# One down-projection over all sixteen token tiles, with seven of its eight tile pairs by Strassen's algorithm

## The chip, the cores and the metric

The kernel runs on one core of a Trainium2 chip. The core has five instruction streams: PE (TensorE, matrix products into the 8 banks of PSUM), DVE (VectorE), ACT (ScalarE), POOL (GpSimd) and SP (SyncE, which issues every DMA here). Work that depends on another stream waits on a semaphore. The metric is the time of one execution on the device in microseconds (us); lower is better. A time is the median of several runs. The profiler records one further execution, and its own time stands beside its span in the table below.

## The reference

The program is one transformer block over 2048 tokens of width 1024: layer norm, a segmented attention with a compressive memory (32 heads, 4 segments of 512 tokens), an output projection, a second layer norm and a gated feed-forward part with 3584 hidden columns.

```python
x = A_x                                        # [1, 2048, 1024]
h = x + _A_ref(_layernorm(x), A_wq, A_wk, A_wv, A_wo, A_beta)
h2 = h + _B_ref(_layernorm(h), B_w1, B_w3, B_w2)

def _B_ref(x, w1, w3, w2):                     # w1, w3: [1024, 3584]; w2: [3584, 1024]
    gate = jnp.einsum('bsd,df->bsf', x, w1)
    up = jnp.einsum('bsd,df->bsf', x, w3)
    h = _silu(gate) * up
    out = jnp.einsum('bsf,fd->bsd', h, w2)
    return out
```

In `_A_ref`, each segment does causal softmax attention within itself, adds what it retrieves from the memory of the earlier segments, and the result goes through `wo`. Inputs and output are bf16.

## The kernel before

The tokens form 16 tiles of 128, and two blocks of 1024 (tiles 0 to 7 and 8 to 15). The 3584 hidden columns form 14 chunks of 256 (`ch`), or 28 groups of 128 (`fc`, or `n` in the second block). `hnT[s]` holds the layer-normed rows of segment s, transposed; `h_scr` in DRAM holds the residual rows `h`, of which a tile is later read back into a buffer `hr`.

Every operation is first noted as an `Op` with its engine, its dependences and a cost; then `schedule` fixes the order on each engine and `emit` writes it out. For the first part of the program the order is a table of numbers (`ORDER`), so written out by hand. `BEHIND` inserts operations behind a numbered one. Operations created while `G.clock` is set are *planned*: they are sorted on their engine by that clock. `LATER` gives such a clock to some operations of the table. A wait is always for what the order and the dependences ask; a stream runs strictly in order.

The stages, with names that come back below:

- **Attention with the first up-projection.** Segments 0 to 3 of the attention are interleaved on TensorE with the up-projection of block 0 (`ffn_up`): per chunk the weights `w1b` and `w3b` are loaded (two buffers of each, used in turn), and four *units* follow, each 16 matmuls of 128x128x512 into two banks. ScalarE takes the gate (`sg`, line 1448), VectorE makes the product in two instructions and writes it to a hidden tile `hm[fc]`, [128, 1024] bf16. The 28 hidden tiles lie in SBUF as `hmA` (25) and `hmB` (3). In between `wo_stage(s)` projects a segment's attention output, adds the residual, does the layer norm and transposes by DMA; `wo_stage(3)` does it for the last segment.
- **First down-projection**, `ffn_down(0, ...)`: 8 token tiles x 2 halves x 28 matmuls = 448, with `w2` resident as `w2a`. Each tile adds `hr` and stores half rows through `ob`.
- **Weight scales**, `weight_scale`, beside it: the second up-projection works with f16 sums of the weights, so it scales w1 and w3 (one number for each) and w2 (one number) by powers of two. For that the squares of all weights are summed: ScalarE squares a piece with `accum_out` into a column of `sq` (`squares`, line 1421), for chunks 8 to 13 from the buffers of the first block, for chunks 0 to 7 from a second load into the `wide` buffers. A matmul with `ones` adds the partitions up, GpSimd takes the power -1/2 (line 1560), and VectorE keeps the exponent and makes the reciprocal (lines 1564 to 1566).
- **Second up-projection**, `products7`, block 1: Strassen's algorithm over 2x2 blocks, so seven products of four matmuls in place of eight, for each of the 28 groups (784 matmuls). `token_sums` makes the sums of the tokens (`S`) once; VectorE makes the sums of the weights (`T`, line 1609) for each group after ScalarE has scaled the chunk (line 1600); GpSimd multiplies w2 by its scale in the meantime (line 1639).
- **Second down-projection**, `down7`: the first pair of token tiles (8 and 9) as in block 0 by 112 matmuls, during which VectorE makes the sums of w2 (`Td`); then three pairs by Strassen's algorithm, 7 x 14 = 98 matmuls each. For each pair VectorE makes four sums of the hidden tiles (`pair_sums`, into `Sd`) and the combinations in `uu`, `ww` and `qq`; `ha` and `hb` are the pair's two residual tiles in `hr`.

The matmul helper `mms` is line 776 and the dense DMA helper line 407 in every view; the layer norm (`ln`) has the square of a whole row block at line 889.

Of the kernel before, what the change touches and what calls it, by code (L numbers as in the profile page):

```python
# [7 lines left out]
AF = mybir.ActivationFunctionType  # L8
# [178 lines left out]
    "6576575675675675675677565107316576556756756756756401646765645112176123477516566067147512"  # L187
    "624046476574174210464562016467")
# [10 lines left out]
    1704: 6.0, 1865: 5.1, 1866: 5.11, 1867: 5.12, 1868: 5.13, 1869: 7.2, 1870: 7.9, 1871: 8.6,  # L199
    1879: 10.5, 1880: 10.51, 1883: 12.6, 1884: 13.3, 1885: 14.0,  # L200
# [4 lines left out]
BEHIND = {8: (1733, 1733), 9: (1749, 1726), 10: (1779, 1756), 11: (1793, 1809), 12: (1832, 1832),  # L205
          13: (1876, 1853)}
# [63 lines left out]
class Graph:  # L270
# [7 lines left out]
    DMA_FIX = 1900.0  # L278

# [143 lines left out]
    def schedule(self):  # L423
# [4 lines left out]
        order = {}  # L428
        for e in ENGINES:
# [12 lines left out]
            order[e] += sorted((o for o in ops if e in o.engs and o.plan is not None),  # L442
                               key=lambda o: (o.plan, o.seq))
# [28 lines left out]
        for _ in self.ops:  # L472
            best = None
            for e in ENGINES:
                if heads[e] == len(order[e]):
                    continue
                o = order[e][heads[e]]
                if any(d not in done for d in o.deps):
                    continue
                t = max([free[e]] + [d.end if d.eng == e == "pe" else done[d] for d in o.deps])  # L480
# [16 lines left out]


# [97 lines left out]
class Kernel:  # L596
# [13 lines left out]
    def plan(self):  # L610
# [80 lines left out]
        for i, off in enumerate((r2, r2 + 8192)):  # L691
# [36 lines left out]
        assert ring >= wo + 6144 + 4096
        self.T = [buf(f"T{i}", [128, 16, 128], F16, ring + 4096 * i) for i in range(2)]
        self.S = [buf(f"S{i}", [128, 4, 512], F16, base[self.hnT[0].name][1] + 4096 * i)  # L730
                  for i in range(4)]
        hn0 = base[self.hnT[0].name][1]
        t1, t2, t4 = (buf(f"Td{i}", [128, 14, 512], F16, hn0 + 14336 * i)[:, :, :]
# [6 lines left out]
                   for i in range(3)]  # L740
        self.hd = g.dram("h_scr", [2048, 1024], BF16)
# [675 lines left out]
    def squares(self, src, n, early=0):  # L1417

        out, to = self.sq[:, n:n + 1], self.junk2[early]
        src, to = (t.rearrange("p c n -> p (c n)") for t in (src, to))  # L1420
        return self.g.op("act", act_ns(2048) + 190, lambda e, gr: [e.activation(
            to, src, AF.Square, accum_out=out)], reads=[src], writes=[to, out])

    def ffn_up(self, blk, ch):
# [468 lines left out]
```

## Time and profile before

| what | value |
|---|---|
| median of 3 runs | 850.92 us (850.85 to 851.23) |
| profiled execution, its own time | 851.94 us |
| its span, first to last instruction | 850.2 us |
| matmuls | 5645 |
| granted TensorE clock | 1.000 |
| bytes moved by DMA | 111.01 MB |
| second up-projection | 590.7 to 759.9 us |
| second down-projection | 759.9 to 847.6 us |

A page of the profile lists the busy time of each engine, the span in slices, the DMA queues, the chain of work that ended last and the costliest groups of instructions. A row of the timeline or of a group reads: start and length in us, engine, line, operation, output<-inputs with their shapes (partitions x elements); where the engine was idle before, the idle time stands in brackets with the instruction that ended it. "PEld" is TensorE's weight load, which runs beside the matmuls. A share of busy time is a mean over stages with different limits; which engine limits a stage is read from that stage. The profiled execution took 1.0 us longer than the median of the runs.

### The profile page before, as it was taken

To read this page: it belongs to the slowest core of one execution; us is meant where nothing else is said; L and a number is where in the kernel's file an instruction comes from. 1 tells how busy PE (TensorE), PEld (TensorE's weight loads), DVE (VectorE), ACT (ScalarE), POOL (GpSimd) and SP (SyncE) were. 2 spreads that over 40 slices of the span, in tenths; PEclk is the share of its full clock that TensorE was granted. 3 is DMA by queue.
4 is the path that set the end of the run, shared out by engine and by line. 5 is a ranking of instruction groups with operands and counts; after the bars stand their busy time and mean duration, and the time that the engine had idled before them with its cause. 6 is when DMAs were issued, how large, how long until landed. Compare 5 with 4: busy or idle time off the path is not lost.

```text
span 850.2 us, 13983 instructions
## 1 busy us (share of the span) xinstructions
PE 845.0 (99%) x5645; PEld 381.7 (45%) x5645; DVE 551.0 (65%) x906; ACT 483.3 (57%) x520; POOL 295.0 (35%) x288
## 2 busy tenths in 40 slices
PE   8999999999999999999999999999999999999998
PEld 5443434444444444444444444444444444444444
DVE  5777886876757677856445522312888888888443
ACT  4878677667757565532343139991777777730000
POOL 1535244425244262510200000001777777750000
DMA  7798966836893626458628279310233323201011
GB/s 235 193 213 207 236 134 182 185 90 179 210 206 91 165 61 165 112 177 217 202 74 236 59 164 304 119 33 25 59 91 99 99 66 85 75 0 51 17 49 59
DMA packets 159663, 111.01 MB, mean 131 GB/s; under 512 B 46832, under 2 KB 145392, under 8 KB 158576
## 3 DMA queue, kind: packets, MB, share of 16 engines
q1 hardware_dynamic: 159600, 110.13, 49.5%
q8 instruction: 44, 0.72, 0.4%
q14 instruction: 19, 0.16, 0.1%
HBM read 90.19 MB, written 9.44 MB: 117 GB/s over the span
## 4 chain that ended last, share of the span: by engine, by line
PE 99%; DMA 1%; SPq 0%; issue 0%; DVE 0%; DVEq 0%
PE ps L776 92%; PE ps L1148 3%; PE ps L1241 3%; DMA wp<-in_A_wk_dram 1%; PE ps L1069 0%; PE ps L1365 0%; SPq L407 0%; PE ps L1234 0%; PE ps L788 0%; DVE ob L1752 0%; DVEq L554 0%
## 5 line engine op out<-in xcount | busy, mean ns | idle before, releaser
L1162 ACT ACTIVATE et<-ps 128x2048 bf16<-128x2048 f32 x80 | 150.1, 1876 | 47.7 <-PE ps L1148 45.8
L776 PE MATMUL ps<-w2a,hmA 128*128 128x512 bf16 (+2 forms) x597 | 129.1, 371 | 0.1
L1171 POOL TENSOR_SCALAR_AFFINE_SELECT et<-et 128x512 bf16<-128x512 bf16 (+1 forms) x96 | 83.0, 876 | 112.3 <-ACT et L1162 112.3
L776 PE MATMUL ps<-hnT,w1b 128*128 128x512 bf16 x448 | 108.1, 379 | 0.0
L776 PE MATMUL ps<-hnT,w3b 128*128 128x512 bf16 x448 | 107.8, 379 | 0.0
L1448 ACT ACTIVATE sg<-ps 128x512 bf16<-128x512 f32 x56 | 33.4, 596 | 97.0 <-PE ps L776 95.7
L776 PEld LDWEIGHTS ps<-w2a,hmA 128*128 128x128 bf16 x597 | 57.5, 98 | 67.1 <-issue 0.5
L1639 POOL TENSOR_SCALAR w2a<-w2a,sc 128x1024 bf16<-128x1024 bf16 x28 | 79.7, 2848 | 7.0 <-PE ps L776 7.0
L776 PE MATMUL ps<-S,T 128*128 128x512 f16 x336 | 81.7, 379 | 0.0
L1451 DVE SCALAR_TENSOR_TENSOR t<-sg,ps 128x512 bf16<-128x512 bf16 x56 | 38.2, 684 | 63.9 <-ACT sg L1448 63.8
L776 PEld LDWEIGHTS ps<-hnT,w1b 128*128 128x128 bf16 x448 | 42.6, 98 | 52.5 <-issue 3.7
L776 PEld LDWEIGHTS ps<-hnT,w3b 128*128 128x128 bf16 x448 | 42.6, 98 | 52.4 <-issue 3.1
L1643 POOL TENSOR_TENSOR c<-uu,ww 128x512 bf16<-128x512 f32 x28 | 45.6, 1628 | 48.9 <-DVE uu L1634 48.9
L776 PE MATMUL ps<-xnT,wp 128*128 128x512 bf16 (+1 forms) x352 | 60.9, 321 | 1.3 <-DMA wp<-in_A_wk_dram 1.3
L776 PE MATMUL ps<-wo,oT 128*128 128x512 bf16 x256 | 61.1, 380 | 0.0
L776 PE MATMUL ps<-hnT,wp 128*128 128x512 bf16 x256 | 59.7, 380 | 0.0
L776 PE MATMUL ps<-hnT,wide 128*128 128x512 bf16 x224 | 57.5, 379 | 0.0
L747 ACT ACTIVATE wide<-wide,sc 128x2048 bf16<-128x2048 bf16 x28 | 55.6, 1991 | 0.0
L776 PEld LDWEIGHTS ps<-S,T 128*128 128x128 f16 x336 | 32.9, 98 | 39.6
L1456 DVE SCALAR_TENSOR_TENSOR hmA<-t,ps 128x512 bf16<-128x512 bf16 x50 | 34.0, 683 | 18.8 <-PE ps L776 18.5
L1187 DVE TENSOR_TENSOR sum<-sum,et 128x512 bf16<-128x512 bf16 (+1 forms) x64 | 40.6, 642 | 6.1 <-POOL et L1171 3.8
L1649 DVE SCALAR_TENSOR_TENSOR cc<-ps,sc,uu 128x1024 bf16<-128x1024 f32 x28 | 35.9, 1284 | 11.2 <-PE ps L776 11.2
(183 smaller groups left out, 1296.3 us busy)
## 6 DMA issues: line engine op xcount, KB each, us to landing
wide<-in_B_w_dram SPq DMA_DIRECT2D x19, 512.0 KB, 4.0
wide<-in_B_w_dram SPq DMA_DIRECT2D x38, 256.0 KB, 4.5
wp<-in_A_wv_dram SPq DMA_DIRECT2D x8, 1024.0 KB, 5.9
wp<-in_A_wq_dram SPq DMA_DIRECT2D x7, 1024.0 KB, 5.5
wp<-in_A_wk_dram SPq DMA_DIRECT2D x7, 1024.0 KB, 7.1
w1b<-in_B_w_dram SPq DMA_DIRECT2D x14, 512.0 KB, 4.9
w3b<-in_B_w_dram SPq DMA_DIRECT2D x14, 512.0 KB, 4.8
w2a<-in_B_w_dram SPq DMA_DIRECT2D x7, 1024.0 KB, 5.8
```

The costliest lines, as they stand in the source:

```text
L747: return self.g.op("act", cost, lambda e, gr: [e.activation(out, in_, func, scale=scale)], reads=reads, writes=[out], cls=cls, **kw)
L776: return [e.matmul(p[0](gr), p[1], p[2], start=p[3], stop=p[4], **kw) for p in part]
L1148: ins.append(e.matmul(self.bank(gr, j, 512 - 128 * kc, off), k[r, g0 + g, 128 * kc:128 * kc + 128], q[r, g0 + g, 128 * kc:512], start=True ...
L1162: return [e.activation(et[:, :, :], src, AF.Exp, scale=self.scale)]
L1171: self.pool_op(lambda e, v=v, pat=pat: e.affine_select(v, v, pattern=pat, compare_op=ALU.is_ge, fill=0.0, base=0, channel_multiplier=-1), ...
L1187: lambda e, gr: [e.tensor_tensor(o, a, b, op=ALU.add) for o, a, b in sums],
L1448: self.g.op("act", act_ns(512), lambda e, gr, sg=sg: [e.activation(sg, self.bank(gr), AF.Tanh, scale=0.5)], writes=[sg], cls=0, group=gg)
L1451: e.scalar_tensor_tensor(t1, sg, 1.0, self.bank(gr), op0=ALU.add, op1=ALU.mult)], reads=[sg], writes=[t1], cls=0,
L1456: e.scalar_tensor_tensor(dst, t1, 0.5, self.bank(gr), op0=ALU.mult, op1=ALU.mult)], reads=[t1], writes=[dst], cls=0,
L1639: self.pool_op(lambda e, w2=w2: e.tensor_scalar(w2, w2, be, None, op0=ALU.mult), 1024, [w2, be], [w2])
L1643: self.pool_op(lambda e: e.tensor_tensor(c22, u, w, op=ALU.add), 512, [u, w], [c22], inputs=2)
L1649: G.op("dve", dve_ns(1024), lambda e, gr, k=k: [e.scalar_tensor_tensor(cc[:, :, :], self.ps[:, (k + 2) * 512:(k + 4) * 512].rearrange("p ( ...
```

## The change

The block order is changed: the up-projections of both blocks come first, then one down-projection over all 16 token tiles.

- **Up-projection of block 0.** Chunks 0 to 7 stay in the table. Chunks 8 to 13 (24 units) are made by `up_unit`, which gives ScalarE a `Silu` and VectorE one multiplication per unit, and the four `wo` tiles of segment 3 are made by `wo_tile` among them. All of this is planned by clock; on the engines but TensorE the planned operations are now picked by `next_of`, a list scheduler that takes what its cost model has ready first, in a window of 48. The clock counts from `zero` = 393.43 us of that model.
- **Scales.** The squares of chunks 0 to 7 are taken in the attention, from `w1b` and `w3b` as they lie there, in 32 instructions of 1024 columns. The second loads for them are gone. There are now 28 scales, one for each chunk of w1 and of w3 (`scales`), made with one matmul, one power and the same VectorE steps over 28 columns, plus `gam` (a common factor) and `ka`, `s2` of 14 columns. They are made ahead of the last three units of the first up-projection. The scale of w2 (`down_scale`) is made ahead of the last unit, from 28 squares of 1024 columns (`down_squares`); chunks 8 to 13 keep their 12 squares of 2048.
- **Second up-projection.** Its hidden tiles are written to a staging tile (`stg`, two buffers) and stored in DRAM (`hm_scr`, 28 stores of 256 KB), since block 0's hidden tiles still occupy SBUF.
- **Down-projection.** `first_pair` does tiles 0 and 1 by 112 matmuls. `scale_pair` multiplies the hidden columns of tile pairs 1 to 3 by `gam` on ScalarE (12 instructions). Seven pairs follow by Strassen's algorithm: tiles 2 to 7 from block 0, 8 to 15 from block 1. At the start of pairs 1 to 4, `reload_pair` brings the hidden columns of a pair of block 1 from `hm_scr` to the place in `hmA`/`hmB` of the pair just done (1.84 MB in rows of 512 bytes).

In all TensorE has 5589 matmuls. Its order is the same as before up to the 3489th.

The diff, cut to its core:

```diff
+BEHIND = {
+    0: (1352, 1352, 1352, 1352), 1: (1403, 1403, 1403, 1403), 2: (1177, 1177, 1433, 1442),
...
+    def next_of(self, ops, free, done, look=48):
+
+        best = []
+        for o in [o for o in ops[:look] if o.plan < self.LOOSE or o.kind == "dma"] or ops[:1]:
+            if all(d in done for d in o.deps):
+                lead = self.LEAD if o.kind == "dma" or max(o.cost.values()) < 1000.0 else 0.5
+                t = max([free, (self.zero + o.plan - lead) * 1e3] + [done[d] for d in o.deps])
+                best.append((t, o))
...
@@ ffn_up
-        if blk == 0 and ch in BEHIND:
-            for b, w in enumerate((w3, w1)):
-                self.squares(w[:, :, :], 2 * ch + b, ch < 13).behind = BEHIND[ch][b]
+        for i, o in enumerate(BEHIND[ch]):
+            w = (w3, w1)[i // 2][:, 4 * (i % 2):4 * (i % 2) + 4, :]
+            self.squares(w.rearrange("p c n -> p (c n)"), self.sq[:, 4 * ch + i:4 * ch + i + 1],
+                         self.junk[:, :]).behind = o
...
+    def up_unit(self, ch, jj, tc, t, banks):
...
+        G.op("act", act_ns(512), lambda e, gr: [e.activation(sg, self.bank(gr), AF.Silu)],
+             writes=[sg], group=gg)
...
+        G.op("dve", dve_ns(512), lambda e, gr: [e.tensor_tensor(dst, self.bank(gr), sg,
+                                                                op=ALU.mult)],
+             reads=[sg], writes=[dst], group=gu)
...
+    def power(self, n2, al, inv, sqb, k, when, bank):
...
+        self.mms(gr, [(lambda gr: self.bank(gr, 0, k), self.ones[:, :], sqb, True, True, k)], 8)
+        G.clock += 0.5
+        G.op("dve", 200.0, lambda e, gr: [e.tensor_scalar(n2, self.bank(gr, 0, k), 1e-30, None,
+                                                          op0=ALU.max)], writes=[n2], group=gr)
+        mh = self.mhalf[:, :].to_broadcast([128, k])
+        self.tiny(lambda e: e.tensor_tensor(n2, n2, mh, op=ALU.pow), [n2, self.mhalf[:, :]], n2,
+                  "pool")
+        ti = n2.bitcast(I32)
+        self.tiny(lambda e: e.tensor_single_scalar(ti, ti, 0x7F800000, op=ALU.bitwise_and), [n2], n2)
+        self.tiny(lambda e: e.tensor_scalar(al, n2, 4096.0, None, op0=ALU.mult), [n2], al)
+        self.tiny(lambda e: e.reciprocal(inv, al), [al], inv)
+
+    def scales(self, when, bank):
...
+        self.power(n2, al, inv, sqb, 28, when, bank)
...
@@ products7
+                G.clock = (at - 42.0, at - 13.6, at)[ch] if ch < 3 else at + 28 * MM * (2 * ch - 4) + 0.4
+                self.load_wide(ch, slot)
...
+            sums(0, 8, W[:, 0:8, :], W[:, 4:12, :], ALU.subtract, t - 1.6 - 2.0 * (n == 0))
...
-                dst = self.hm[n][:, 512 * i:512 * i + 512]
+                dst = stg[:, 512 * i:512 * i + 512]
...
+            G.clock = t + 28 * MM + 3.2
+            G.dma(self.hmd[128 * n:128 * n + 128, :], stg[:, :])
...
+    def scale_pair(self, p, t, gam):
+
+        c = slice(256 * p, 256 * p + 256)
+        for h, lo, hi in ((self.hmA, 0, 9), (self.hmA, 9, 18), (self.hmA, 18, 25), (self.hmB, 0, 3)):
+            v = h[:, lo:hi, c]
+            self.g.clock = t
+            self.act(v, v, AF.Copy, act_ns(256 * (hi - lo), 1), scale=gam, extra=[gam])
+            t += 2.2
+
+    def reload_pair(self, p, t):
+
+        c = slice(256 * p, 256 * p + 256)
+        src = self.hmd.rearrange("(f p) n -> p f n", p=128)
+        n = self.hmA.shape[1]
+        self.g.clock = t
+        self.g.dma(self.hmA[:, :, c], src[:, 0:n, c])
+        self.g.dma(self.hmB[:, :, c], src[:, n:28, c])
...
@@ down7
-        self.ffn_down(1, at, inv, 2)
+        self.first_pair(at, inv0)
...
         for p in range(1, 4):
+            self.scale_pair(p, at + 10.0 * (p - 1), gam)
+        for p in range(1, 8):
             t = at + 112 * MM + 98 * MM * (p - 1)
+            if p < 5:
+                self.reload_pair(p - 1, t + 0.5)
...
@@ tail
+        gam, ig = self.scales(items[-3][0] - 0.01, items[-2][2][0])
+        be, ib, inv = self.down_scale(items[-1][0] - 0.01, items[-4][2][0], ig)
+        self.token_sums(64.0)
+        self.products7(end, be)
+        self.down7(end + 28 * 28 * MM, ib, inv, gam)
```

How the order of instructions moves shows at three places. The rows name line, operation, output<-inputs and shape.

First, ScalarE in the last segment of the attention (`et` is an exponential, `sg` a gate, `kT` a key tile). Before:

```order
L799 ACTIVATE kT_81<-ps 128x512
L1448 ACTIVATE sg_121<-ps 128x512 x2
L1448 ACTIVATE sg_122<-ps 128x512
L1162 ACTIVATE et_92<-ps 128x2048
L1162 ACTIVATE et_93<-ps 128x2048
```

And after:

```order
L842 ACTIVATE kT_81<-ps 128x512
L1490 ACTIVATE sg_121<-ps 128x512
L1462 ACTIVATE junk,sq<-w3b_118 128x1024 x2
L1462 ACTIVATE junk,sq<-w1b_117 128x1024 x2
L1490 ACTIVATE sg_121<-ps 128x512
L1490 ACTIVATE sg_122<-ps 128x512
L1205 ACTIVATE et_92<-ps 128x2048
L1205 ACTIVATE et_93<-ps 128x2048
```

Four squares of a chunk's weights now stand between its first gate and its second, and so ahead of the next exponential; the other chunks have theirs in other such places.

Second, VectorE where the scales are made. Before, among the tiles of the first down-projection (`ob` is an output half, `S` a token sum):

```order
L1556 TENSOR_SCALAR sc<-ps 128x2
L1579 TENSOR_TENSOR S_155<-hnT_115,hnT_116 128x2048
L1564 TENSOR_SCALAR sc<-sc 128x2
L1565 TENSOR_SCALAR sc<-sc 128x2
L1566 RECIPROCAL sc<-sc 128x2
```

And after, among the last units of the first up-projection:

```order
L1567 TENSOR_SCALAR sc<-ps 128x28
L1525 TENSOR_TENSOR hmB<-ps,sg_122 128x512
L1525 TENSOR_TENSOR hmB<-ps,sg_121 128x512
L1573 TENSOR_SCALAR sc<-sc 128x28
L1574 TENSOR_SCALAR sc<-sc 128x28
L1575 RECIPROCAL sc<-sc 128x28
L1590 TENSOR_REDUCE sc<-sc 128x2
L1592 SCALAR_TENSOR_TENSOR sc<-sc 128x1
L1594 RECIPROCAL sc<-sc 128x1
L1596 TENSOR_SCALAR sc<-sc 128x14
L1598 SCALAR_TENSOR_TENSOR sc<-sc 128x14
L1525 TENSOR_TENSOR hmB<-ps,sg_122 128x512
```

The scale steps went from 2 columns to 28 and from the middle of the down-projection to the last units before the second up-projection; the product of the last unit but one (the row at the end) stands behind them, and the first sum of weights T follows three rows later.

Third, SP's queue in a Strassen pair of the down-projection, before:

```order
L407 DMA hr_128<-h_scr 128x1024
L407 DMA hr_129<-h_scr 128x1024
L407 DMA out_dram<-ob_131 128x512
L407 DMA out_dram<-ob_132 128x512
L407 DMA out_dram<-ob_133 128x512
L407 DMA out_dram<-ob_134 128x512
L407 DMA hr_130<-h_scr 128x1024
```

And after:

```order
L420 DMA hmA<-hm_scr 128x25x256
L420 DMA hmB<-hm_scr 128x3x256
L420 DMA out_dram<-ob_134 128x512
L420 DMA hr_129<-h_scr 128x1024
L420 DMA out_dram<-ob_131 128x512
L420 DMA out_dram<-ob_132 128x512
L420 DMA out_dram<-ob_133 128x512
```

The two reloads stand at the head of the pair, and a residual tile that the same pair reads follows behind them.

More of the change, by code (lines that the diff above doesn't have):

```diff
@@ L427, in schedule @@
         ops = [o for o in self.ops if o.behind is None]
-        order = {}
+        order, ahead = {}, {}
         for e in ENGINES:
@@ L474, in schedule @@
             for e in ENGINES:
[L475 to L480, printed above, removed]
+                if heads[e] < len(order[e]):
+                    o = order[e][heads[e]]
+                    if any(d not in done for d in o.deps):
+                        continue
+                    t = max([free[e]] + [d.end if d.eng == e == "pe" else done[d] for d in o.deps])
+                else:
+                    t, o = self.next_of(ahead.get(e, ()), free[e], done)
+                    if o is None:
+                        continue
                 if best is None or t < best[0]:
@@ L484, in schedule @@
             e = o.eng
+            if heads[e] == len(order[e]):
+                order[e].append(o)
+                ahead[e].remove(o)
             heads[e] += 1
@@ new lines, in down_scale @@
+    def down_scale(self, when, bank, ig):
+        G = self.g
+        sc = self.sc
+        n2, be, ib, i1, raw = (sc[:, a:a + 1] for a in (116, 118, 119, 120, 150))
+        parts = sc[:, 152:180]
+        sqb = self.sqb[:, 0:1]
+        G.clock = when - 1.0
+        self.dve_op(lambda e: e.tensor_reduce(raw, parts, mybir.AxisListType.X, ALU.add), 200.0,
+                    [parts], [raw])
+        self.tiny(lambda e: e.tensor_copy(sqb, raw), [raw], sqb)
+        self.power(n2, be, ib, sqb, 1, when, bank)
+        self.tiny(lambda e: e.tensor_tensor(i1, ib, ig, op=ALU.mult), [ib, ig], i1)
+        return be, ib, i1
@@ L1797, in down7, with down_squares @@
                 give(None, q2[:, c0:c0 + n], 0, c0, 6 * L + L * (c0 + n) / 512 + 0.3, gr, n)
+    def down_squares(self):
+        for i in range(28):
+            self.g.clock = 26.0 + 2.2 * i
+            self.squares(self.w2a[:, i, :], self.sc[:, 152 + i:153 + i], self.junk[:, :])
     def tail(self):
-        self.down_weights()
-        self.g.first_planned = len(self.g.ops)
-        down = 8 * 56 * MM
-        al, inv, ka, s2, be, inv2 = self.weight_scale(0.0)
-        self.token_sums(50.0)
@@ L1806, in tail @@
-        self.ffn_down(0, 0.0)
-        self.products7(down, al, inv, ka, s2, be)
-        self.down7(down + 28 * 28 * MM, inv2)
-        self.g.clock = None
+        G = self.g
+        U = 16 * MM
+        one = self.ones[:, :]
+        G.clock = -1.0
+        self.pool_op(lambda e: e.memset(one, 1.0), 128, [], [one])
+        pairs = [(5, 7), (4, 6), (5, 7)] + 7 * [(0, 2), (1, 3), (4, 6), (5, 7)]
+        t, n = 8 * MM, 0
+        start, items = {}, []
+        for j in range(24):
+            if j == 1:
+                t += 0.35
+            if j == 3:
+                t = 16.0
+            items.append((t, (8 + j // 4, j % 4), pairs[n]))
+            start.setdefault(8 + j // 4, t)
+            t, n = t + U, n + 1
+            if 5 <= j <= 8:
+                items.append((t, j - 5, pairs[n]))
+                t, n = t + U, n + 1
@@ L1827, in run @@
                 self.wo_stage(s)
-        for ch in range(14):
+        for ch in range(8):
             self.ffn_up(0, ch)
```

319 lines of the change are left out of this document (180 added, 139 removed), and 10 rows, old and new, of tables (BEHIND, LATER).

## The prediction

> **What bounds the kernel now.** I read the page first (the span, the busy times, the chain that ended last), then TensorE's timeline for its cadence, then the busy times of each engine by stage.
>
> ```profile
> span 850.2 us, 13983 instructions
> PE 845.0 (99%) x5645; PEld 381.7 (45%) x5645; DVE 551.0 (65%) x906; ACT 483.3 (57%) x520; POOL 295.0 (35%) x288
> PE 99%; DMA 1%; SPq 0%; issue 0%; DVE 0%; DVEq 0%
> ```
>
> TensorE is busy 99% and the chain is TensorE for 99%. Busy alone proves little, so the cadence decides:
>
> ```profile
> 487.66 1.03 PE L776 MATMUL ps<-hnT,w1b 128*128 128x512 bf16 x4
> 488.76 1.46 PE L776 MATMUL ps<-w2a,hmA 128*128 128x512 bf16 x6
> ...
> 759.89 2.32 PE L776 MATMUL ps<-w2a,hmA 128*128 128x512 bf16 x10
> ...
> 784.07 3.18 PE L776 MATMUL ps<-Td,Sd 128*128 128x512 f16 x14
> ...
> 805.22 1.03 PE L776 MATMUL ps<-Td,Sd 128*128 128x512 f16 x4
> ```
>
> From 759.89 to 784.07 the first pair of token tiles runs its 112 matmuls in 24.18 us; from 784.07 to 805.22 the next pair runs Strassen's 98 in 21.15. Both are 0.216 us a matmul, bf16 or f16: no gaps. The one gap near the change is at 488.76: four matmuls from 487.66 end their turn at 488.53, so 0.23 us were lost where the first down-projection begins.
>
> ```profile
> core 0: us, PE busy (x) PEld busy (x) DVE busy (x) ACT busy (x) POOL busy (x), PEclk, DMA share, GB/s
> 200.00:393.00 193.00, 193.00 (x1619) 84.56 (x1618) 130.63 (x218) 115.23 (x121) 72.00 (x86) 1.00 0.62 153
> 393.00:488.00 95.00, 95.00 (x456) 42.89 (x454) 49.40 (x81) 31.68 (x42) 10.13 (x15) 1.00 0.54 153
> 488.00:590.70 102.70, 102.63 (x479) 46.37 (x477) 25.21 (x51) 70.97 (x70) 6.98 (x8) 1.00 0.50 132
> 590.70:759.90 169.20, 169.20 (x786) 76.69 (x785) 142.20 (x222) 121.79 (x136) 121.78 (x55) 1.00 0.26 73
> 759.90:784.10 24.20, 24.20 (x114) 11.00 (x113) 21.38 (x19) 1.30 (x2) 0.00 (x0) 1.00 0.14 39
> 784.10:847.60 63.50, 63.50 (x323) 30.29 (x321) 28.71 (x40) 3.58 (x6) 5.35 (x3) 1.00 0.14 42
> ```
>
> By stage: attention with the first up-projection, its end, the first down-projection, the second up-projection, the plain pair, three Strassen pairs. TensorE is full in each, at granted clock 1.00. So TensorE work taken out is time taken out, unless a new wait appears.
>
> **The change, part by part.**
>
> *Matmuls.* Token tiles 2 to 7 and 10 to 15 make six Strassen pairs, 8 and 9 the seventh, 0 and 1 stay plain. Before, 0 to 9 were plain. Four pairs go from 24.18 to 21.15 us: 4 x 3.03 = 12.1 us off TensorE, which is 56 matmuls. The 0.23 us at 488.76 belong to a stage that is gone. TensorE's order is the same, matmul for matmul, up to 391 us. Sum: 12.3 us.
>
> *Squares of the weights, chunks 0 to 7.* They leave ScalarE's 488 to 569 us stretch (with 5 MB of second loads for them) and become 32 squares of 1024 columns in the attention. A square of that size is a 1.05 us instruction and its read, next start 1.17 us later:
>
> ```profile
> 212.73 1.05 ACT L889 ACTIVATE junk<-h 128x1024 bf16<-128x1024 bf16 x1
> 213.68 0.19 ACT L889 ACTIVATION_READ_ACCUMULATOR junk<-h 128x1 f32 x1
> 213.90 0.20 ACT L747 ACTIVATE lnst<-lnst 128x1 f32<-128x1 f32 x1
> ...
> 298.59 0.60 ACT L1448 ACTIVATE sg<-ps 128x512 bf16<-128x512 f32 x1 [2.14 <-PE ps L776]
> ...
> 318.37 1.88 ACT L1162 ACTIVATE et<-ps 128x2048 bf16<-128x2048 f32 x1 [1.09 <-PE ps L1148]
> ```
>
> I laid all 14 groups of squares on the gaps where they now stand. The worst are the two quoted: two squares (2.35) in a gap of 2.14, one (1.18) in 1.09; the overruns of all groups add to 0.45 us, behind which a bank of PSUM is waited for at the earliest. Bounds 0 and 0.45 us; I take 0.2, since no row shows TensorE waiting for ScalarE there. The squares also hold weight buffers longer: chunk 7's w1 load moves from 358 to about 368 us and is read at 379.
>
> *ScalarE from 393 us to the second up-projection.* 24 gates, 12 squares of 2048 columns and 28 of 1024:
>
> ```profile
> L1448 ACT ACTIVATE sg<-ps 128x512 bf16<-128x512 f32 x56 | 33.4, 596 | 97.0 <-PE ps L776 95.7
> ...
> 540.55 1.91 ACT L1421 ACTIVATE junk<-w2a 128x2048 bf16<-128x2048 bf16 x1
> 542.36 0.18 ACT L1421 ACTIVATION_READ_ACCUMULATOR junk<-w2a 128x1 f32 x1
> 542.58 1.91 ACT L1421 ACTIVATE junk<-w2a 128x2048 bf16<-128x2048 bf16 x1
> ```
>
> 24 x 0.60 + 12 x 2.03 + 28 x 1.18 = 72 us of 102 (24 units and 4 output tiles of 16 matmuls, less what stands before 393). It fits, with the last squares queued until some 4 us before they are needed. Cost 0; were that cover gone, each us late is a us of TensorE.
>
> *The scale chain: the part I cannot see.* Before, two scales were made in the middle of the down-projection, 40 us before use. Now 28 are made three units (48 matmuls, 10.4 us) before the products that need them, and GpSimd's power runs over 28 columns.
>
> ```profile
> 549.19 0.17 PE L776 MATMUL ps<-sqb,ones 128*128 128x2 bf16 x1
> ...
> 549.43 0.16 DVE L1556 TENSOR_SCALAR sc<-ps 128x2 f32<-128x2 f32 x1
> 549.50 1.22 DVE L1579 TENSOR_TENSOR S<-hnT,hnT 128x2048 f16<-128x2048 bf16 x1
> 551.31 0.17 DVE L1564 TENSOR_SCALAR sc<-sc 128x2 int32<-128x2 int32 x1 [0.59 <-POOL sc L1560]
> 551.51 0.17 DVE L1565 TENSOR_SCALAR sc<-sc 128x2 f32<-128x2 f32 x1
> ...
> 549.67 1.61 POOL L1560 TENSOR_TENSOR sc<-sc,mhalf 128x2 f32<-128x2 f32 x1 [56.52 <-DVE sc L1556]
> ...
> 568.90 5.77 ACT L747 ACTIVATE wide<-wide,sc 128x2048 bf16<-128x2048 bf16 x3
> ...
> 667.59 0.68 DVE L1609 TENSOR_TENSOR T<-wide 128x1024 f16<-128x1024 bf16 x1
> ...
> L949 POOL TENSOR_TENSOR rstd<-lnve,mhalf 128x1 f32<-128x1 f32 x4 | 2.2, 555 | 9.8 <-DVE lnve L948 9.8
> L933 POOL TENSOR_SCALAR lnve<-lnmv 128x1 f32<-128x1 f32 x22 | 5.5, 250 | 93.6 <-DVE lnmv L906 87.7 <-DVE T L1280 5.8
> ...
> 71.96 1.12 DVE L1187 TENSOR_TENSOR sum<-et,et 128x1024 bf16<-128x1024 bf16 x1
> 72.52 0.99 POOL L936 TENSOR_TENSOR rstd<-lnve,mhalf 128x1 f32<-128x1 f32 x1
> ```
>
> Matmul to power 0.48, power P, two VectorE steps 0.40, two ScalarE passes over the first weights 3.85 (5.77 / 3 each), the sum 0.68, hand-overs 0.3 (estimated from the 0.08 between VectorE's end at 549.59 and GpSimd's start): 5.7 + P. It is hidden while P is under 4.65 us. One column takes 0.56. The two-column row says 1.61, which would be 1.05 a further column and P = 28.9. But a VectorE instruction with two inputs ran until 550.72, and the one-column power at 72.52 was stretched to 0.99 by another that ended at 73.08. Counted from those ends, one column needs 0.43 and two need 0.56: 0.13 a column, P = 0.56 + 27 x 0.13 = 4.1, and 0.55 us to spare. Bounds for P: 0.56 and 28.9; I take 4.1, since two rows give the same kind of end. Cost 0.
>
> The Trainium skill, GPSIMD Engine Reference, Key points, says that GpSimd shares its SBUF interfaces with VectorE and contends with its instructions of two SBUF inputs. By that rule the wait in the 1.61 is contention and the sum is 838.8; without it, 863. The same page (Elementwise — side-by-side cycle accounting) has GpSimd loop over the elements in software, against this change: its 2.6 cycles are for an add, and no run here shows a power of more than two columns.
>
> *Second up-projection.* Same instructions; results go to a staging tile and to DRAM, 28 stores of 256 KB in 169 us that moved 73 GB/s. Cost 0. VectorE (84% busy) is the cover that is thin, and gains no work.
>
> *Down-projection.* ScalarE rescales three pairs in 12 passes: by the 1.92 us of 2048 columns about 21 us, in the plain pair, where it was busy 1.30 of 24.2. VectorE's work there is the same 21.4. Each Strassen pair gives VectorE 45% and GpSimd one add. New are four reloads of 1.84 MB, which SP issues ahead of a residual tile that the same pair needs:
>
> ```profile
> 816.16 1.41 DVE L1765 SCALAR_TENSOR_TENSOR qq<-uu,sc,hr 128x512 f32<-128x512 f32 x2
> 817.51 0.69 DVE L1742 TENSOR_TENSOR ww<-ps,ww 128x512 f32<-128x512 f32 x1
> ...
> DMA packets 8253, 4.49 MB, mean 300 GB/s; under 512 B 206, under 2 KB 8010, under 8 KB 8253
> hr<-h_scr SPq DMA_DIRECT2D x1, 256.0 KB, 5.3
> ```
>
> Weights in rows of the same 512 bytes moved at 300 GB/s (503 to 518 us). Reload and two residual tiles, 2.36 MB, take 7.9 us; with 0.6 to issue and the 4.4 that the loaded queue added to a tile (5.3 less 0.9), they land by 12.9 us into the pair. VectorE reads the tile at 11.7 (816.9 in a pair begun at 805.2), and TensorE needs VectorE's next add, now done at 818.2, by 820.3: 2.1 us of room, so by 13.8. Cost 0. The end of the program is unchanged.
>
> *Sum.* The profiled execution took 851.94 us (span 850.2 and 1.7 around it), 1.0 above the median of 850.92. 12.3 off gives 839.6 for it, 838.6 for the median; with 0.2 for the squares, **838.8**.
>
> **Rivals.**
>
> 1. *The power costs what its first column seems to: 0.31* (0.56 less 0.25 for a plain one-column operation). P = 8.9, TensorE waits 4.3 us before the products: 843.1. For it: software, no row over two columns. Against: the two ends above.
> 2. *Slower: the power costs 1.05 a column.* TensorE waits 28.9 - 4.65 = 24.3 us: 863. It decides above 0.61 us a column (P = 17). For it: the bare 1.61. Against: the 0.99 of one column.
> 3. *The reload holds up pairs 2 to 4.* At 200 GB/s the tile lands at 16.8, 3 us late in three pairs: 848. Likelier a part of it, 840 to 844. Against: 300 GB/s measured with the queue full.
> 4. *ScalarE or weight loads late before the second up-projection:* 840 to 844.
> 5. *No gain,* if several waits meet: within 0.2% (1.7 us, about what a measurement of this kernel can tell from no change).
>
> **How the numbers follow.** Forecast (838.0 to 839.8) 0.58; rival 1 0.15; rival 2 0.05; rival 3 0.09; rival 4 0.09; rival 5 0.04. Below 849.2: 0.91; within: 0.04; above: 0.05. A range from 838.0 to 844.0 holds the forecast, rival 1 and most of 3 and 4, 0.88 in all; less would cut the bound of P that I trust least.
>
> **What would show it.** 5589 matmuls and TensorE busy about 833; the power over 28 columns near 4 us, and no idle before the first matmul on T; ScalarE's groups in the attention without a later exponential; no gap in pairs 2 to 4. I am wrong if TensorE waits for VectorE at the first product, or if its cadence in the pairs is over 21.2 us.

## The result and the profile after

The changed kernel takes 839.95 us in the median (839.42 to 840.60, 4 runs), the kernel before 851.07 us beside it: a ratio of 0.987, 95% interval 0.9853 to 0.9887. The forecast was 838.8, in a range from 838.0 to 844.0. The profiled execution took 839.42 us, its span is 837.6.

First the page of after, the span and the busy times:

```profile
span 837.6 us, 13935 instructions
PE 825.6 (99%) x5507; PEld 376.4 (45%) x5589; DVE 567.6 (68%) x924; ACT 513.4 (61%) x600; POOL 307.1 (37%) x293
```

The weight loads (PEld) count 5589 matmuls as foreseen; 82 matmul records are missing, so busy 825.6 is too small and says nothing of gaps.

The two spans differ by 12.6 us, more than the 11.1 of the medians. Where, three rows of TensorE's timeline tell: the first product with a loaded weight, the last sums of the attention (the same matmul in both), and the last matmuls of all. Before:

```profile
9.58 1.07 PE L776 MATMUL ps<-xnT,wp 128*128 128x128 bf16 x16 [1.25 <-DMA wp<-in_A_wk_dram]
...
371.17 0.23 PE L1241 MATMUL ps<-et,ones 128*32 128x128 bf16 x4
...
847.42 0.33 PE L776 MATMUL ps<-w2a,hmB 128*128 128x128 bf16 x3
```

And after:

```profile
8.51 1.07 PE L819 MATMUL ps<-xnT,wp 128*128 128x128 bf16 x16 [0.69 <-DMA wp<-in_A_wk_dram]
...
370.02 0.23 PE L1284 MATMUL ps<-et,ones 128*32 128x128 bf16 x4
...
834.85 0.33 PE L819 MATMUL ps<-w2a,hmB 128*128 128x128 bf16 x3
```

Of the 12.6 us, 1.07 lie ahead of the first product, where both have the same code and wait for the first loads. From there to the last sums it is 361.59 before and 361.51 after, although 27 of the 32 squares now stand between (the other five follow, the last at 378.4). What the change did is in the **last part**, from the row at 370 to the row at 835: 476.25 before, 464.83 after, 11.42 less.

The Strassen pairs are as forecast. TensorE in the plain pair of after and the first Strassen pair, each row the first of a run:

```profile
662.72 5.56 PE L819 MATMUL ps<-w2a,hmA 128*128 128x512 bf16 x24
...
686.89 3.19 PE L819 MATMUL ps<-Td,Sd 128*128 128x512 f16 x14
...
708.04 2.32 PE L819 MATMUL ps<-Td,Sd 128*128 128x512 f16 x10
```

24.17 and 21.15 us, the same as before. But there is one wait that the forecast does not have, ahead of the last unit of the first up-projection. The timeline of after, engine by engine:

```profile
482.70 4.80 POOL L1570 TENSOR_TENSOR sc<-sc,mhalf 128x28 f32<-128x28 f32 x1 [29.77 <-DVE sc L1567]
...
487.54 0.18 DVE L1573 TENSOR_SCALAR sc<-sc 128x28 int32<-128x28 int32 x1 [3.72 <-POOL sc L1570]
...
488.92 0.68 DVE L1525 TENSOR_TENSOR hmB<-ps,sg 128x512 bf16<-128x512 f32 x1
...
489.73 0.16 DVE L1612 CAST sqb<-sc 128x1 bf16<-128x1 f32 x1
491.96 0.69 DVE L1666 TENSOR_TENSOR T<-wide 128x1024 f16<-128x1024 bf16 x1 [2.08 <-ACT wide L790]
...
487.41 1.89 PE L819 MATMUL ps<-hnT,w3b 128*128 128x512 bf16 x8
490.03 0.16 PE L819 MATMUL ps<-sqb,ones 128*128 128x1 bf16 x1 [0.73 <-ACT wide L790]
...
493.50 1.03 PE L819 MATMUL ps<-S,T 128*128 128x512 f16 x4
```

Eight matmuls from 487.41 end their turn at 489.14; the next, the sum for the scale of w2, starts at 490.03: 0.89 us lost. The row names ScalarE's pass over the weights. Its operand `sqb`, however, is written by VectorE's conversion (CAST), which ends at 489.89, and that stands in VectorE's queue behind the whole chain of 28 scales, whose power took 4.80. The first product on T, at 493.50, waits for nothing. With this the last part closes: 56 x 0.2159 = 12.09 and the 0.23 of the vanished stage, less 0.89, is 11.43; measured 11.42.

### The profile page after: what moved, and what is told of

Its sections match the earlier page's. It is cut to its first block, busy times and chain, and to the rows that moved or that the text cites. A ratio compares the mean times of both kernels' runs of the same rounds, so it can differ in the third digit from the quotient of the medians.

```text
span 837.6 us, 13935 instructions
## 1 busy us (share of the span) xinstructions
PE 825.6 (99%) x5507; PEld 376.4 (45%) x5589; DVE 567.6 (68%) x924; ACT 513.4 (61%) x600; POOL 307.1 (37%) x293
## 4 chain that ended last, share of the span: by engine, by line
PE 95%; DMA 1%; issue 1%; ACT 1%; POOL 1%; SPq 0%; DVE 0%; ACTq 0%; DVEq 0%
PE ps L819 88%; PE ps L1191 3%; PE ps L1284 3%; DMA wp<-in_A_wk_dram 1%; DMA w3b<-in_B_w_dram 1%; POOL sc L1570 1%; ACT junk L1462 0%; PE ps L1112 0%; PE ps L1408 0%; SPq L420 0%; ACT wide L790 0%; ACT et L1205 0%; PE ps L1277 0%; PE ps L831 0%; DVE t L1493 0%
## 5 line engine op out<-in xcount | busy, mean ns | idle before, releaser
L819 PE MATMUL ps<-hnT,w1b 128*128 128x512 bf16 x437 | 106.4, 379 | 0.9 <-issue 0.5
L1845 ACT ACTIVATE ww<-ps 128x512 f32<-128x512 f32 x7 | 4.2, 597 | 113.3 <-PE ps L819 113.3
L1891 POOL TENSOR_TENSOR ww<-uu,ww 128x512 f32<-128x512 f32 x7 | 13.5, 1932 | 152.1 <-DVE ww L1850 152.1
L819 PE MATMUL ps<-w2a,hmA 128*128 128x512 bf16 (+2 forms) x288 | 61.5, 363 | 0.4
L819 PE MATMUL ps<-wo,oT 128*128 128x512 bf16 x247 | 59.1, 379 | 1.0 <-issue 0.8
L819 PE MATMUL ps<-S,T 128*128 128x512 f16 x224 | 57.5, 379 | 0.0
L819 PE MATMUL ps<-hnT,T 128*128 128x512 f16 (+1 forms) x222 | 57.2, 379 | 0.1
L819 PE MATMUL ps<-hnT,wide 128*128 128x512 bf16 x212 | 55.1, 379 | 0.6
L819 PE MATMUL ps<-Td,Sd 128*128 128x512 f16 x196 | 44.6, 379 | 0.0
L1706 DVE SCALAR_TENSOR_TENSOR cc<-ps,sc,uu 128x1024 bf16<-128x1024 f32 x28 | 35.9, 1284 | 11.1 <-PE ps L819 11.1
L819 PE MATMUL ps<-w2a,Sd 128*128 128x512 f16 (+1 forms) x190 | 43.1, 379 | 0.3
```

The costliest lines, as they stand in the source:

```text
L819: return [e.matmul(p[0](gr), p[1], p[2], start=p[3], stop=p[4], **kw) for p in part]
L1706: G.op("dve", dve_ns(1024), lambda e, gr, k=k: [e.scalar_tensor_tensor(cc[:, :, :], self.ps[:, (k + 2) * 512:(k + 4) * 512].rearrange("p ( ...
L1891: self.pool_op(lambda e: e.tensor_tensor(ww, u, ww, op=ALU.add), 512, [u, ww], [ww], inputs=2)
```

## The experiments

The last part (from the row at 370 to the row at 835) is the measure throughout: it is free of the start, and came out at 464.83, 464.82 and 464.82 us in three profiles of kernels that leave it alone (after, as_changed, power_sizes). Two expectations below call the row at 370 "matmul 3489"; by the count of weight loads it is matmuls 3386 to 3389, and their 361.5 and 467.5 us are counted from that row. Each ratio is to runs of the kernel before made beside it (medians 851.07 to 851.62).

| kernel | median us | ratio to before (interval) | last part, us |
|---|---|---|---|
| before | 851.07 | | 476.25 |
| after | 839.95 | 0.987 (0.9853 to 0.9887) | 464.83 |
| as_changed | 840.25 | 0.9868 (0.9854 to 0.9883) | 464.82 |
| scales_early | 840.97 | 0.9877 (0.9862 to 0.9892) | 465.38 |
| cast_first | 840.00 | 0.987 (0.9854 to 0.9887) | 464.42 |
| power_twice | 847.96, one run | | 472.52 |
| chain_early | 839.37 | 0.986 (0.9846 to 0.9875) | 463.93 |
| power_sizes | 839.01, one run | | 464.82 |
| reload_more | 840.83 | 0.9879 (0.9864 to 0.9894) | 464.83 |
| reload_behind | 845.85 | 0.9931 (0.9914 to 0.9947) | 468.46 |
| pair_plain | 845.15 | 0.9927 (0.991 to 0.9943) | 469.88 |
| pair_plain2 | 842.92 | 0.9895 (0.9881 to 0.991) | 467.85 |
| squares_twice | 877.47, one run | | 479.75 |

**as_changed**: the changed kernel once more.

> The changed kernel once more, for the spread of its time and a second profile. Theory: the two profiled executions of before and after differ by 1.07 us within the first 10 us, where both have the same code (the first product with wp starts at 9.58 and at 8.51); that is the spread of the start. So a new profile may start anywhere between 8.4 and 9.7, but from that product on it has the same length as after within 0.2 us, with one wait of 0.9 us ahead of the last unit of the first up-projection (490.03 in after). Rival: the start is faster in the changed kernel; then it is at 8.5 again and the time is 839.4.

The first product came at 8.96, the last sums at 370.26 and the last part was the same to 0.01 us, wait included. The stretch between the two rows was 0.21 us shorter than in after, a little more than the 0.2 expected. So the start and the attention vary by themselves. Over all these profiles the first product lies between 8.51 and 10.30, and the part from there to the row at 370 takes 361.18 to 362.90 (squares_twice apart), while the last part repeats to 0.01. An effect of 0.9 us can therefore be told by the trace and not by the times.

**scales_early**: the 28 scales one unit earlier.

```diff
-        gam, ig = self.scales(items[-3][0] - 0.01, items[-2][2][0])
+        gam, ig = self.scales(items[-4][0] - 0.01, items[-3][2][0])
```

> The matmul that adds up the squares of w1 and w3 stands one unit (16 matmuls, 3.45 us) earlier; its input is ready at 475.95 in after and it would start at 478.7. Theory (the chain of 28 scales is late): the wait of 0.9 us ahead of the last unit goes and nothing takes its place, since the first weight sums T are then ready some 3.4 us before the first product; 0.9 us less than the changed kernel, so 839.0. Rival: the two ScalarE passes over the first weights (3.9 us), which now run ahead of two gates, hold a bank of PSUM and TensorE waits there instead: no gain, 839.9.

Neither: the wait grew, by 0.55 us in the last part. The rival's pass ahead of a gate is in it, but TensorE waits for the conversion and not for a bank. ScalarE, VectorE and TensorE ahead of the last unit:

```profile
488.21 1.99 ACT L790 ACTIVATE wide<-wide,sc 128x2048 bf16<-128x2048 bf16 x1
490.11 1.07 ACT L1521 ACTIVATE sg<-ps 128x512 bf16<-128x512 f32 x2
...
490.72 0.69 DVE L1525 TENSOR_TENSOR hmB<-ps,sg 128x512 bf16<-128x512 f32 x1 [1.68 <-ACT sg L1521]
...
491.54 0.16 DVE L1612 CAST sqb<-sc 128x1 bf16<-128x1 f32 x1
...
491.84 0.17 PE L819 MATMUL ps<-sqb,ones 128*128 128x1 bf16 x1 [1.28 <-DVE sqb L1612]
```

The chain is done earlier, but the conversion is now queued behind a unit's product that waits for a gate, and the gate stands behind a pass over the weights. TensorE waits for the place in VectorE's queue, not for the power as such.

**cast_first**: only the conversion is moved ahead of the chain in VectorE's queue.

```diff
-        G.clock = when - 1.0
+        G.clock = when - 6.5
         self.dve_op(lambda e: e.tensor_reduce(raw, parts, mybir.AxisListType.X, ALU.add), 200.0,
```

> The scales stay where they are; only VectorE's two steps that prepare the sum for the scale of w2 (the reduction and the conversion at 489.52 and 489.73 in after) are queued ahead of its scale steps. Theory A: TensorE's wait at 490.03 is for that conversion, queued behind the chain; it goes, and the first product on T waits some 0.1 to 0.3 us instead (T ends at 492.65, the first product could start at 492.61): 0.6 to 0.8 us less, 839.2. Theory B, as the row of the trace names it: the wait is for ScalarE's pass over the weights; it stays, 839.9.

Theory A: the wait is gone, though ScalarE's pass is where it was, so the releaser named by the row was the wrong one. The gain is smaller than A said, 0.41 us. Rows of TensorE and VectorE at the first products:

```profile
492.68 1.04 PE L819 MATMUL ps<-S,T 128*128 128x512 f16 x4
...
496.21 1.02 PE L819 MATMUL ps<-hnT,T 128*128 128x512 bf16 x3
497.38 1.04 PE L819 MATMUL ps<-S,wide 128*128 128x512 f16 x4
...
494.73 1.00 DVE L1614 TENSOR_TENSOR sc<-sc 128x1 f32<-128x1 f32 x1
...
496.59 0.73 DVE L1691 SCALAR_TENSOR_TENSOR ww<-ps,sc,ww 128x512 f32<-128x512 f32 x1
```

0.09 us are lost at 492.68 (the matmuls before end their turn at 492.59), 0.07 at 496.21 and 0.31 at 497.38, where a bank is read out late by VectorE (496.59), which had its 1-column steps for w2 in between. In after, the 0.89 had covered these: 0.89 less 0.47 is 0.42, and 0.41 came out.

**power_twice**: the power over 28 columns computed twice, the first into scratch.

```diff
+        if k == 28:
+            other = self.sc[:, 122:150]
+            self.tiny(lambda e: e.tensor_tensor(other, n2, mh, op=ALU.pow),
+                      [n2, self.mhalf[:, :]], other, "pool")
```

> GpSimd computes the power over 28 columns twice, the first time into scratch, ahead of the one that is used. Theory A (a power over 28 columns costs 4.8 us by itself, 0.16 a column, and the chain has no room left): TensorE's wait ahead of the last unit grows from 0.9 by 4.8, to 5.7 us, and the second power takes 4.8. Theory B (0.13 a column, and the rest of the 4.80 was contention with VectorE's two products that ran until 483.8): the power that runs while VectorE is idle takes 3.7 to 4.1 and the wait grows by that. Rival C (there is room behind the conversion): the wait grows by less than 3 us.

GpSimd and TensorE:

```profile
483.67 4.80 POOL L1572 TENSOR_TENSOR sc<-sc,mhalf 128x28 f32<-128x28 f32 x1 [29.77 <-DVE sc L1567]
488.55 4.79 POOL L1574 TENSOR_TENSOR sc<-sc,mhalf 128x28 f32<-128x28 f32 x1
...
488.37 1.89 PE L819 MATMUL ps<-hnT,w3b 128*128 128x512 bf16 x8
495.86 0.16 PE L819 MATMUL ps<-sqb,ones 128*128 128x1 bf16 x1 [5.60 <-ACT wide L790]
495.89 3.57 PE L819 MATMUL ps<-hnT,w1b 128*128 128x512 bf16 x8
```

Theory A: 4.79 for a power while VectorE is idle, and a wait of 5.76 (495.86 less 490.10) in place of 0.89, 4.87 more. The last part grew by 7.69, though: eight matmuls take 3.57 instead of 1.89. After the wait 13 of them stood 0.427 us apart instead of 0.216; these 12 spacings and the two at their ends (0.381 and 0.337) are 2.82 us more, and 4.87 + 2.82 is the 7.69.

**chain_early**: scales one unit earlier, the scale of w2 two units earlier with its conversion ahead of the chain (the edit of cast_first), and the scheduler told what the power costs.

```diff
-        gam, ig = self.scales(items[-3][0] - 0.01, items[-2][2][0])
-        be, ib, inv = self.down_scale(items[-1][0] - 0.01, items[-4][2][0], ig)
+        gam, ig = self.scales(items[-4][0] - 0.01, items[-3][2][0])
+        be, ib, inv = self.down_scale(items[-3][0] - 0.01, items[-4][2][0], ig)
...
-        self.tiny(lambda e: e.tensor_tensor(n2, n2, mh, op=ALU.pow), [n2, self.mhalf[:, :]], n2,
-                  "pool")
+        G.clock += 0.2
+        G.op("pool", 400.0 + 157.0 * k, lambda e, gr: [e.tensor_tensor(n2, n2, mh, op=ALU.pow)],
+             reads=[n2, self.mhalf[:, :]], writes=[n2], cls=4)
```

> Three edits together: the 28 scales one unit earlier, the scale of w2 two units earlier with its preparation ahead of the chain, and the list scheduler told what the power takes (0.4 + 0.157 us a column in place of 0.21), so that it queues the gates' products ahead of VectorE's wait for it. Theory (VectorE's queue in the last 12 us before the products is the bound: chain, conversion, 1-column steps and the sums T meet there): with 3.4 us more room and the 1-column steps out of 493 to 496, neither the wait at the last unit nor the waits of cast_first at 492.2, 495.7 and 496.6 (0.3, 0.2, 0.5) remain; 0.9 to 1.0 us less than the changed kernel from the first product with wp to the end. Rival: ScalarE is the bound there (two passes of 1.95 over the first weights between the gates): a wait of 0.5 us or more stays before the first products or in their first 4 us.

Neither wait remains, as the theory said. TensorE's rows, from the last unit into the products:

```profile
490.37 1.89 PE L819 MATMUL ps<-hnT,w1b 128*128 128x512 bf16 x8
492.10 1.89 PE L819 MATMUL ps<-hnT,w3b 128*128 128x512 bf16 x8
493.82 1.03 PE L819 MATMUL ps<-S,T 128*128 128x512 f16 x4
494.69 1.03 PE L819 MATMUL ps<-hnT,T 128*128 128x512 f16 x4
```

1.73 for eight, 0.86 for four, without a gap; the last part is 463.93, 0.90 less than after. Counted from the first product with `wp`, as the expectation has it, the gain is only 0.08, because the stretch ahead of the row at 370, which the edits leave alone, came out 0.82 us longer in this profile (TensorE waited 0.54 for a load of `wp` at 128.32). By the last part it is the fastest version; the times (839.37 and, in as_changed, 840.25) differ in that sense, but less than they vary. Which of the three edits gave how much, no run here separates.

**power_sizes**: powers on scratch in the Strassen pairs.

```diff
+            for k, when in {1: ((1, 9.4),), 2: ((1, 3.6), (2, 4.6)), 3: ((14, 3.6),),
+                            4: ((28, 3.6),), 5: ((28, 9.4),), 6: ((7, 3.6),), 7: ((56, 1.0),)}[p]:
...
+                self.pool_op(lambda e, y=y, mh=mh: e.tensor_tensor(y, y, mh, op=ALU.pow), 600,
+                             [y, self.mhalf[:, :]], [y], inputs=2)
```

> Adds powers of 1, 2, 7, 14, 28 and 56 columns on scratch to GpSimd in the Strassen pairs, where it is idle, each behind a copy by VectorE that sets its start: quiet (VectorE idle) for 1, 2, 7, 14, 28 and 56, and once more for 1 and 28 while VectorE makes sums of two SBUF inputs. Theory A (0.16 a column, nothing else): 0.55, 0.7, 1.5, 2.6, 4.8, 9.2 quiet, and in company longer by the time in which VectorE's two-input sums run. Theory B (0.13 a column; the 4.80 had 0.7 of contention in it): 4.1 for 28 and 7.7 for 56. The time of the kernel is not changed by more than 0.5 us.

GpSimd's rows:

```profile
696.76 1.34 POOL L1885 TENSOR_TENSOR sc<-sc,mhalf 128x1 f32<-128x1 f32 x1 [34.55 <-DVE sc L1882]
...
711.84 0.55 POOL L1885 TENSOR_TENSOR sc<-sc,mhalf 128x1 f32<-128x1 f32 x1 [10.11 <-DVE sc L1882]
712.66 0.70 POOL L1885 TENSOR_TENSOR sc<-sc,mhalf 128x2 f32<-128x2 f32 x1 [0.28 <-DVE sc L1882]
...
733.08 2.60 POOL L1885 TENSOR_TENSOR sc<-sc,mhalf 128x14 f32<-128x14 f32 x1 [10.24 <-DVE sc L1882]
...
754.23 4.79 POOL L1885 TENSOR_TENSOR sc<-sc,mhalf 128x28 f32<-128x28 f32 x1 [10.24 <-DVE sc L1882]
...
781.39 5.57 POOL L1885 TENSOR_TENSOR sc<-sc,mhalf 128x28 f32<-128x28 f32 x1 [16.25 <-DVE sc L1882]
...
814.70 9.27 POOL L1885 TENSOR_TENSOR sc<-sc,mhalf 128x56 f32<-128x56 f32 x1 [7.25 <-DVE sc L1882]
```

Theory A: quiet, 0.39 and 0.159 for each column. The first and the sixth row began during a sum of two SBUF inputs on VectorE (1.08 us) and took 0.79 and 0.78 longer. The expectation has them longer by the time in which VectorE's two-input sums run, and that failed: beside the 28 columns ran another such sum (`Sd` at 784.15, 1.08 us) and two `qq` of two SBUF inputs (from 782.22), and the power took no longer for them. Only the sum during which it began counted. So the 1.61 of two columns before was 0.70 and a wait, and the rival of 863 us is dead.

**reload_more** and **reload_behind**: another copy of each reload's bytes, from DRAM to DRAM.

```diff
-        self.g.dma(self.hmB[:, :, c], src[:, n:28, c])
+        again = self.g.dma(self.hmB[:, :, c], src[:, n:28, c])
+        self.g.dma(self.hmd2.rearrange("(f p) n -> p f n", p=128)[:, :, c], src[:, :, c],
+                   deps=tuple(again.deps))
```

(`deps` is only in reload_behind; without it the scheduler put the copy ahead of the reload.)

> Behind each of the four reloads (1.84 MB) stands a copy of the same 1.84 MB from DRAM to DRAM, ahead of the residual tile, so the DMA queue has twice the bytes there. Theory: in after the tile landed 10 us into the pair and TensorE needs it by 13.8; at 290 GB/s the copy adds 6.3 us to the landing, 16.4, so TensorE waits 2.6 us in each of pairs 1 to 4: 10 us in all, 850. Rival A (the queue serves the tile beside the copy, not behind it): less than 2 us. Rival B (a copy from DRAM to DRAM is slower than a load, 200 GB/s): 9.2 us later, 5.4 in each pair, 22 in all, 862.

The copy went out 5 to 16 us ahead of the reload, not behind it. In pair 2 VectorE waited 1.65 us for the residual tile, until 13.3 us into the pair (724.55 less 711.22; the next expectation has 12.8, from a coarser start), and TensorE lost nothing: 464.83. So it tested less than it was to.

> As reload_more, with the extra copy issued right behind each reload and ahead of the residual tiles (in reload_more it was issued 5 us ahead of the reload, the tile landed 12.8 us into the pair, VectorE waited 1.65 us and TensorE not at all). Theory (what lands by 13.8 us into the pair costs nothing, each us beyond it costs a us): 3.7 MB at 290 GB/s ahead of the tile make it land at about 16.4, so TensorE waits 2 to 3 us in each of pairs 1 to 4: 8 to 12 us in all. Rival: TensorE has more room than 13.8, by the order in which VectorE takes its work: under 2 us in all.

VectorE's waits for the tile, and TensorE's that follow:

```profile
725.04 0.75 DVE L1876 SCALAR_TENSOR_TENSOR qq<-uu,sc,hr 128x512 f32<-128x512 f32 x1 [4.06 <-DMA hr<-h_scr]
...
746.84 0.75 DVE L1876 SCALAR_TENSOR_TENSOR qq<-uu,sc,hr 128x512 f32<-128x512 f32 x1 [2.65 <-DMA hr<-h_scr]
...
768.92 0.75 DVE L1876 SCALAR_TENSOR_TENSOR qq<-uu,sc,hr 128x512 f32<-128x512 f32 x1 [2.93 <-DMA hr<-h_scr]
...
726.45 2.55 PE L820 MATMUL ps<-Td,hmA 128*128 128x512 f16 x11 [1.88 <-DVE ww L1853]
748.25 2.55 PE L820 MATMUL ps<-Td,hmA 128*128 128x512 f16 x11 [0.47 <-DVE ww L1853]
770.33 2.55 PE L820 MATMUL ps<-Td,hmA 128*128 128x512 f16 x11 [0.75 <-DVE ww L1853]
```

The pairs began at 709.30, 732.51 and 754.31, so the tile came 15.74, 14.33 and 14.61 us into them, and they took 23.21, 21.80 and 22.07 in place of 21.15: 2.06, 0.65 and 0.92 lost. Each time the difference is 13.7, which is the limit. The sum is 3.63, less than the 8 to 12 expected, since the tile landed sooner than 16.4 and pair 1 did not wait at all.

**pair_plain** and **pair_plain2**: token tiles 2 and 3 made plain again.

```diff
-        for i in range(2):
-            hr = self.hr[i]
+        for i in range(4):
+            hr = self.hr[i % 3]
...
-        for p in range(1, 8):
-            t = at + 112 * MM + 98 * MM * (p - 1)
+        for p in range(2, 8):
+            t = at + 224 * MM + 98 * MM * (p - 2)
```

> Token tiles 2 and 3 are made plain again, by 112 matmuls in place of Strassen's 98, with their four rescaling passes and VectorE's sums gone. Theory (only the number of matmuls counts, and the work beside them is hidden): 14 matmuls of 0.216, so 3.0 us more than the changed kernel, 842.9 to 843.3. Rival (Strassen's pairs lose time at their ends or through their sums and reloads): less than 2.5 us more.

5.05 us more, so neither number. VectorE, then TensorE, at the first Strassen pair:

```profile
708.26 2.03 DVE L1807 TENSOR_TENSOR w2a<-w2a 128x3584 f16<-128x3584 bf16 x1 [24.73 <-PE ps L819]
...
714.40 3.19 PE L819 MATMUL ps<-Td,Sd 128*128 128x512 f16 x14 [1.86 <-DVE Sd L1789]
```

The edit itself had made this: the sum t3 overwrites a part of w2, so it had to wait for the second plain pair, and everything behind it on VectorE waited too.

> As pair_plain, with VectorE's sum t3 (it overwrites a part of w2 that the plain tiles still read) planned behind the second plain pair instead of the first. In pair_plain it stood at the head of VectorE's queue for 24.7 us and held the first sums Sd back, for which TensorE waited 1.9 us. Theory: without that wait a plain pair costs its 14 further matmuls and no more: 3.0 us more than the changed kernel between matmul 3489 and the last (467.5 there), 470.5. Rival: the wait of 1.9 belongs to the step from a plain to a Strassen pair, wherever t3 stands: 472.5.

467.85 in the last part (the expectation counts to the last record of the weight-load stream at the end of the program, 2.7 us later, so its 467.5 stands for 464.83): 3.02 more, 14 x 0.2159. A plain pair costs its matmuls and nothing else.

**squares_twice**: each square in the attention made twice.

```diff
+            for again in range(2):
+                x = self.squares(w.rearrange("p c n -> p (c n)"),
+                                 self.sq[:, 4 * ch + i:4 * ch + i + 1], self.junk[:, :])
+                x.behind = o
+                if again:
+                    x.cost = {"act": 0.0}
```

(The cost 0 hides the second square from the scheduler.)

> Each of the 32 squares in the attention is made twice (37.8 us more of ScalarE between 255 and 371 us, where it idles some 20%). Theory (the squares stand in gaps that they fill, so the second ones push the exponentials): sliding ScalarE's instructions in the trace of after by 1.18 for each square makes the exponentials up to 8.8 us late by 347; matmul 3489 comes 5 to 9 us later than in the changed kernel (361.5 after the first product with wp). Rival (the order leaves TensorE enough other work at each place): under 1.5 us.

From the first product to the last sums it took 383.78, 22.3 more: more than the theory. VectorE's list of waits over the whole run, the largest row:

```profile
DVE t L1497 <- ACT sg L1494: 50.8, 24, 6.7
```

Gates come late on ScalarE and the products on VectorE behind them; TensorE's largest entry names these products (13.2 us in 5 waits, 8.9 in 4 of them ahead of the last sums). For the exponentials, which the theory names, it waited 0.6 us there, once, and 6.4 us in 2 waits for `Nsb`, another result of ScalarE: the delay came mostly by other ways than the theory's. (The order of its later stages changed as well, so its last part is no measure.) The single squares cost nothing; twice as many cost 22 us. Why 22 and not 5 to 9 is not shown.

## Why the prediction was right, and where it was wrong

- **Matmuls: right.** 56 matmuls, 12.09 us; the single pair, undone, gives 3.02. The lost 0.23 went with its stage.
- **Squares: right, at the lower bound.** 0.2 was taken, and the cost is 0. The first square stands at 249.9 us in after. A row of TensorE ahead of it, before and after:

```profile
225.43 0.40 PE L1234 MATMUL ps<-pq,zsel 128*32 128x512 bf16 x4
...
224.28 0.40 PE L1277 MATMUL ps<-pq,zsel 128*32 128x512 bf16 x4
```

From there to the last sums it is 145.74 us in both; the -0.08 arose ahead of it. The five squares behind the last sums cost nothing either, since the last part closes without them.
- **ScalarE, stores, second up-projection, rescaling: right.** No wait of TensorE stands there in after.
- **Reloads: right, but the landing was put too late.** 13.8 us into the pair was the limit forecast, 13.7 is measured. The landing was forecast at 12.9; in pair 2 of after the second residual tile landed at 10.65 (718.69 less 708.04), and VectorE read it at 11.6 (forecast 11.7) without a wait.
- **The scale chain: wrong, by 0.89 us.** The step said that the chain is hidden while the power takes less than 4.65, took 4.1 for it, and set the cost at nothing. Two things failed. The power takes 4.80: two rows stretched by contention gave 0.13 a column, where the quiet rows give 0.159. And the step priced one reader, the first product on T. That one indeed did not wait in after, where the 0.89 came ahead of it; with that wait gone, in cast_first, it waited 0.09, and the step's own sum with 4.80 gives 0.15. So one of the signs named beforehand, no idle before the first matmul on T, came true and did not show the fault. But the chain also holds VectorE's queue, and in it stood the conversion for the scale of w2, which TensorE needs 3.45 us earlier. cast_first and chain_early show this cause. An estimate from these rows: with 4.1 the conversion would have ended 0.7 us sooner, and TensorE would have waited some 0.2. So the reader left out costs 0.2 by itself and the longer power 0.15; it took both for 0.89.

The median lies 1.15 us above the forecast; 0.89 is this wait, less 0.2 for the squares. The remaining 0.46 is within the 1.2 us over which the times of the changed kernel spread. At 839.95 the median is just outside the forecast's own band (838.0 to 839.8). It is inside the range because that was drawn up to 844.0 for a dearer power, the bound that the prediction trusted least: the mechanism and the main term held, and the doubt was in the right place.

Of the rivals, the first had the right cause (a power dearer than 4.1) at five times the price, and put the wait at the products, not ahead of the last unit. What the Trainium skill says on contention (GPSIMD Engine Reference, Key points), by which the forecast set the 1.61 aside, agrees: 0.55 quiet, 1.34 beside a sum of two SBUF inputs.

## What to carry to other kernels

Price a chain for everyone who stands behind it: list what is queued after it on each engine that it crosses, and when the bound engine needs each of those, not only the chain's own result. When a wait is removed, look for what it had covered: cast_first gave 0.41 of 0.89, and moving the chain alone made it worse, until queue and chain were moved together. A cost that the scheduler doesn't know (0.21 us for a power of 4.80) can become an order in which engines wait.

## What the runs showed of the hardware

TensorE lost speed after long waits: after 5.60 us of idle in power_twice 13 matmuls stood 0.427 us apart in place of 0.216, so a wait of 5.76 us cost 2.8 more. The granted clock there was 0.50 (495.9 to 501.3 us). Rows of TensorE in squares_twice show the edge:

```profile
261.80 1.45 PE L819 MATMUL ps<-hnT,w3b 128*128 128x512 bf16 x6 [3.58 <-DVE t L1497]
...
341.76 0.53 PE L1191 MATMUL ps<-qT,kT 32*128 32x512 bf16 x4 [3.66 <-ACT Nsb L1337]
342.22 1.89 PE L819 MATMUL ps<-hnT,w1b 128*128 128x512 bf16 x4
...
366.95 1.86 PE L819 MATMUL ps<-hnT,w3b 128*128 128x512 bf16 x4 [3.93 <-DVE t L1497]
```

Six matmuls in 1.45 after 3.58 us of idle are at full speed; four in 1.89 after 3.66 and four in 1.86 after 3.93 are not. The Trainium skill, TensorE: Matmul & The Clock Gate, section HAM oscillation — how this bites in real kernels, puts the edge at gaps over about 3.4 us; these rows put it between 3.58 and 3.66. Whether it always lies there, three waits cannot tell.

An instruction of VectorE with one column took 1.00 us (494.73 in cast_first, and the same in after and chain_early) where its neighbours take 0.15 to 0.17, while GpSimd began a pass over w2 at 494.60. What holds it, no run here tells apart.
